# An attention and feed-forward kernel: late query pairs head by head, one first-layer tile later, early query tails in one slot

## The chip, the cores and the metric

The kernel runs on one core of a Trainium2 chip. The metric is the time of one execution in microseconds on the device; several runs are taken and the median is given. TensorE (PE in the profile) multiplies matrices, VectorE (DVE) and ScalarE (ACT) work on elements, GpSimd (POOL) only fills a few tiles here, and SyncE (SP) issues nearly all DMAs from one queue, in order.

## The reference

Two parts in a row: a kernelised attention over 8 batches, 8 heads, 576 tokens and 64 dimensions, then a gated feed-forward layer (FFN) over the 4608 tokens with 512 model dimensions and 1536 hidden ones.

```python
def phi(x):
    proj = np.einsum('bhsd,df->bhsf', x, w_phi)                     # 64 -> 128
    proj = proj - np.max(np.abs(proj), axis=-1, keepdims=True)
    return np.concatenate([np.exp(proj), np.exp(-proj)], axis=-1)   # 256 features
q_p, k_p = (phi(q), phi(k))
kv = np.einsum('bhsf,bhsd->bhfd', k_p, v)
z = np.sum(k_p, axis=2)
num = np.einsum('bhsf,bhfd->bhsd', q_p, kv)
den = np.einsum('bhsf,bhf->bhs', q_p, z)[..., None] + 1e-06
x = (num / den)  # heads side by side: [4608, 512]
g = x @ w_gate
out = (g * (1.0 / (1.0 + np.exp(-g)))) * (x @ w_val) @ w_out
```
Everything is float32. w_gate, w_val and w_out arrive as float64.

## The kernel before

**Attention** goes by pairs of heads: 32 pairs (8 batches, 4 pairs each), made by `attention(i, rank)`. The first 8 are "early": they multiply in plain float32, keep queries with tokens on the partitions, and are double-buffered. The other 24 are "late" (`split`): each float32 operand is taken apart into a rounded part and a remainder (`qh`, `ql`, `kvh`, `kvl`), and there is one set of their buffers.

- Keys: 576 tokens are four tiles of 128 and a rest of 64. `K_GROUPS` makes two groups of two tiles and a tail. In the tail both heads' last 64 tokens share one tile of 128 columns: head 0's rows stand in the first 64 columns, head 1's in the last 64, the rest of `kin` is zero there, and the weight `wst` (w_phi twice, one above the other) projects it to 128 features.
- Early queries: `SLOTS` lists five tiles, and the last starts at token 448, so it takes 64 tokens a second time. Each tile is projected with `wbd` (w_phi twice on the diagonal, 256 columns, both heads), L284; VectorE takes the largest magnitude (L477) and subtracts it (L482), TensorE turns it (L493, one block per head and tile), ScalarE makes the two exponentials (L504).
- Late queries stay features by tokens: rounded part and remainder (L513, L515), projection per head, copies (L528), a 32x32 transpose per head (L533). From there on both heads go in one step: the maximum (L537), six small steps that carry it over the partition groups (L540 to L545), its spreading by a transpose (L549), the subtraction (L551), two exponentials (L553, L554), the rounded copies `qh` (L564) and the remainders `ql` (L567).
- Numerators: products of the query features with `kvs` or `kvh`, `kvl`, in four pieces (two parts of 288 tokens, two heads), copied by L592 and L594, then divided (L601 to L605) and laid into the FFN's input `xh`, `xl` (L617, L619).

**FFN** goes by chunks c of 384 tokens (12) and hidden tiles f of 128 (12). `first(c, f)` is one first-layer tile: 24 products into the two banks `gv` (L284), tanh (L700), two VectorE steps (L702, L705). `parts` makes `hh` and `hl` (L725, L726). `second(c, f)` is 9 products into the three banks `o` (L284); after f = 11 each bank is copied to one of two `osb` buffers (L766) and stored. Chunks 0 to 2 (`EARLY`) share one pass over the weights: for each f, `first` of all three chunks; chunk 0's `second` follows at once, put off by one tile (`put_off` holds one `second` back and issues the one before), and the results of chunks 1 and 2 go to DRAM (`keep`, L712) and come back later (`fetch`, L717). The low parts of w_out for those two chunks are loaded into buffers that the first layer no longer needs (`low_parts_at_rest`, L650).

The weights are turned from float64 into two parts by `weight_piece` (L304 to L325), 36 pieces, on VectorE and ScalarE.

**Order.** Every step is given to a planner (`Plan`) with an engine, a cost, what it waits for and a rank. It runs through time on these costs and issues each engine's instructions in the order in which they would start, lowest rank first; hardware queues keep that order. FFN products have the last rank on TensorE and are chained one after the other in the code's order (`product`); the FFN's steps on the other engines have the first rank. Weights' pieces rank at 3.0, 5.0 and 6.5 to 7.6, pair i at i. Where TensorE has nothing in the plan, it gets a product of zeros (L817 to L821), until chunk 0's last `second` is issued.

Of the kernel before, what the change touches and what calls it, by code (L numbers as in the profile page):

```python
# [29 lines left out]

SLOTS = [0, 128, 256, 384, 448]
Q_GROUPS = [(0, 2), (2, 4), (4, 5)]

K_GROUPS = [(0, 2), (2, 4), (4, 5)]
SK = 5 * P
# [133 lines left out]
def dve(n):  # L169
    return 150 + 1.04 * n  # L170
# [14 lines left out]
def pe32(n):  # L185
    return 2 * max(112, 0.85 * n)
# [3 lines left out]
def favor_attention_moe(ctx: ExitStack, tc: tile.TileContext, qT, kT, v, w_phi, wg, wv, wo, out):  # L190
# [80 lines left out]
    for h in range(2):  # L271
        nc.gpsimd.memset(vf[0][h * D:(h + 1) * D, 4, 1 - h], 0.0)
        nc.gpsimd.memset(kin[0][h * D:(h + 1) * D, 4 * P + (1 - h) * D:4 * P + (2 - h) * D], 0.0)

# [68 lines left out]
    def attention(i, rank):  # L343
# [6 lines left out]
        sets = 2 if early else 1  # L350
        use = lambda name: [last.get((name, i - sets))]

# [27 lines left out]
        kv_steps = []  # L380
        for g, (t0, t1) in enumerate(K_GROUPS):

# [80 lines left out]
        if early:  # L463
            for g, (t0, t1) in enumerate(Q_GROUPS):
# [4 lines left out]
                view = lambda key=key, w=w: work[plan.bank[key]][:, :w * 256].rearrange("p (t f) -> p t f", f=NF)  # L469

                def project(t0=t0, t1=t1, key=key):
# [4 lines left out]
                pj = add("PE", w * pe32(256), project, [q_in], rank, take=key)  # L476
                mx = add("DVE", dve(256 * w), lambda w=w, m=m, view=view: vec.tensor_reduce(  # L477
                    out=m[:, 4:4 + 2 * w], in_=view(), axis=AX.X, op=ALU.max, apply_absolute_value=True),
                    [pj, last.get(("qm", n - len(km)))], rank)

                def centre(w=w, m=m, view=view, y=y):
                    vec.tensor_tensor(  # L482
                        out=y[:, :2 * w], in0=view(), op=ALU.subtract,
                        in1=m[:, 4:4 + 2 * w].rearrange("p (n o) -> p n o", o=1).broadcast_to([P, 2 * w, NF]))

                qc = add("DVE", dve(256 * w), centre, [mx, last.get(("qy", n - 2))], rank, give=key)
                last["qm", n] = qc

                def turn(w=w, y=y, key2=key2):
                    o = work[plan.bank[key2]]  # L490
                    for h in range(2):
                        for t in range(w):
                            nc.tensor.transpose(o[:, (h * w + t) * P:(h * w + t + 1) * P], y[:, 2 * t + h], ident)  # L493

                tn = add("PE", 2 * w * 108, turn, [qc], rank, take=key2)
                last["qy", n] = tn

                skip = P - (S - 4 * P) if t1 == len(SLOTS) else 0
                size = w * P - skip

                def exponential(k, t0=t0, w=w, skip=skip, size=size, key2=key2):
                    x = work[plan.bank[key2]][:, :2 * w * P].rearrange("p (h s) -> p h s", h=2)[:, :, skip:]
                    at = SLOTS[t0] + skip
                    nc.scalar.activation((qe, qx)[k][j][:, :, at:at + size], x, AF.Exp, scale=-1.0 if k else 1.0)  # L504

                f0 = add("ACT", act(2 * size), lambda f=exponential: f(0), [tn, *use("qe"), *use("qx")], rank)
                f1 = add("ACT", act(2 * size), lambda f=exponential: f(1), [f0], rank, give=key2)
            last["qin", i] = pj
        else:
            copies, q_lo = [], []  # L510
            for h in range(2):
                ra, rb = rows(h)
                hi = add("ACT", act(S), lambda h=h, ra=ra: nc.scalar.copy(q_parts()[ra, h], qin[j][ra]),  # L513
                         [q_in, last.get(("qs", h, i - 1)), *first_late("qx", "qe")], rank)
                lo = add("DVE", dve(S), lambda h=h, ra=ra, rb=rb: vec.tensor_tensor(  # L515
                    out=q_parts()[rb, h], in0=qin[j][ra], in1=q_parts()[ra, h], op=ALU.subtract), [hi], rank)
                q_lo.append(lo)
                for part in range(2):
                    key = ("q", i, h, part)
                    c = slice(part * SH, (part + 1) * SH)  # L520

                    def project(h=h, c=c, key=key):
                        acc = work[plan.bank[key]][:, :SH]
                        x = q_parts()[:, h, c]
                        matmuls([(acc, wst_hi, x, True, False), (acc, wst_lo, x, False, True)])

                    pj = add("PE", 2 * pe(SH), project, [lo], rank, take=key)
                    copies.append(add("ACT", act(SH), lambda h=h, c=c, key=key: nc.scalar.copy(  # L528
                        qx[j][:, h, c], work[plan.bank[key]][:, :SH]), [pj, *use("qx")], rank, give=key))
                last["qs", h, i] = pj  # L530
# [4 lines left out]

            def largest():
                vec.tensor_reduce(out=qm, in_=blocks(qe[j]), axis=AX.X, op=ALU.max, apply_absolute_value=True)  # L537

            def over_groups():
# [9 lines left out]
            back = add("DVE", dve(2 * S), lambda: vec.transpose(  # L549
                blocks(qe[j]), qu.rearrange("p (a o) -> p a o", o=1).broadcast_to([P, 2 * NBL, 32])), [mg], rank)  # L550
            qc = add("DVE", dve(2 * S), lambda: vec.tensor_tensor(out=flat(qx[j]), in0=flat(qx[j]), in1=flat(qe[j]),  # L551
                                                                  op=ALU.subtract), [back], rank)
            f0 = add("ACT", act(2 * S), lambda: nc.scalar.activation(flat(qe[j]), flat(qx[j]), AF.Exp), [qc], rank)  # L553
            f1 = add("ACT", act(2 * S), lambda: nc.scalar.activation(flat(qx[j]), flat(qx[j]), AF.Exp, scale=-1.0), [f0], rank)  # L554

        done = [f1]
        if split:
            done = []
            for k in range(2):
                part = (qe, qx)[k][j]  # L560

                def rounded(k=k, part=part):
                    take_over()
                    nc.scalar.copy(flat(qh[k]), flat(part))  # L564

                g0 = add("ACT", act(2 * S), rounded, [(f0, f1)[k], last.get(("nu", i - 1)), *weights_done], rank)
                done += [g0, add("DVE", dve(2 * S), lambda k=k, part=part: vec.tensor_tensor(  # L567
                    out=flat(ql[k]), in0=flat(part), in1=flat(qh[k]), op=ALU.subtract), [g0, f1], rank)]


        copied = []
# [28 lines left out]
        wide = lambda t: t.rearrange("p (a j) -> p a j", j=32)  # L600
        t0 = add("DVE", dve(S), lambda: vec.transpose(turned, den), [*copied, *done], rank)  # L601
        t1 = add("DVE", 260, lambda: vec.reciprocal(rc, wide(turned)[:, :, 0]), [t0], rank)
# [3 lines left out]
        last["qe", i] = t1  # L606
        last["qx", i] = done[-1] if split else nu

# [264 lines left out]
```

## The time and the profile before

| | |
|---|---|
| median of 3 runs | 1282.01 us (1281.12 to 1282.61) |
| the profiled execution | 1281.95 us |
| its span, first to last instruction | 1280.2 us |
| mean granted TensorE clock | 0.996 |
| instructions | 19566 |
| TensorE, weight loads, VectorE, ScalarE busy | 1265.3, 1191.8, 869.2, 642.2 us |
| bytes moved by DMA | 168.13 MB, 131 GB/s |

The profile is of one execution. Times in its rows are us from the span's start unless marked ns. A row of a group of instructions gives line, engine, operation, output and inputs by the program's names, shapes, count, then the total busy time in us and the mean in ns of one, then the engine's idle time before them and what ended it. A row of the timeline gives start, length, engine and line, and in brackets the idle time before it and what ended that. TensorE's products overlap: the length of one is more than the distance to the next, so a cost on TensorE is the distance of two starts. Line numbers are those of the listing above.

### The profile page before, as it was taken

To read this page: it belongs to the slowest core of one execution; us is meant where nothing else is said; L and a number is where in the kernel's file an instruction comes from. 1 tells how busy PE (TensorE), PEld (TensorE's weight loads), DVE (VectorE), ACT (ScalarE), POOL (GpSimd) and SP (SyncE) were. 2 spreads that over 40 slices of the span, in tenths; PEclk is the share of its full clock that TensorE was granted. 3 is DMA by queue.
4 is the path that set the end of the run, shared out by engine and by line. 5 is a ranking of instruction groups with operands and counts; after the bars stand their busy time and mean duration, and the time that the engine had idled before them with its cause. 6 is when DMAs were issued, how large, how long until landed. Compare 5 with 4: busy or idle time off the path is not lost.

```text
span 1280.2 us, 19566 instructions
## 1 busy us (share of the span) xinstructions
PE 1265.3 (99%) x7440; PEld 1191.8 (93%) x7440; DVE 869.2 (68%) x1554; ACT 642.2 (50%) x1287; POOL 1.2 (0%) x11
## 2 busy tenths in 40 slices
PE   9999999999999999999999999999999999999998
PEld 8897899999889999999999999999999999999998
DVE  7998999998787777762777787742477877322222
ACT  5877433336676666531656665531455565221211
POOL 0000000000000000000000000000000000000000
PEclk9999999999899999999999999999999999999999
DMA  5443355543564434444433443444444442443443
GB/s 146 123 121 99 126 179 176 173 163 120 170 195 149 121 102 119 135 126 124 142 107 106 115 140 106 123 151 123 122 129 118 112 132 86 123 148 124 148 123 107
DMA packets 110829, 168.13 MB, mean 131 GB/s; under 512 B 51472, under 2 KB 58128, under 8 KB 110736
## 3 DMA queue, kind: packets, MB, share of 16 engines
q1 hardware_dynamic: 110272, 166.63, 43.6%
q8 instruction: 58, 0.95, 0.3%
q14 instruction: 35, 0.29, 0.1%
q10 hardware_dynamic: 464, 0.26, 0.1%
HBM read 143.26 MB, written 23.59 MB: 130 GB/s over the span
## 4 chain that ended last, share of the span: by engine, by line
PE 93%; DVE 5%; ACT 1%; issue 1%; DMA 1%; SPq 0%; DVEq 0%
PE gv L284 47%; PE o L284 25%; PE work L284 12%; PE kv L431 8%; PE kv L424 1%; PE o L493 0%; DVE kp L411 0%; DVE qy L482 0%; DMA shared<-in_wg_dram 0%; DVE km L406 0%; DVE km L477 0%; DVE qe L549 0%; DVE hl L726 0%; DMA wbd<-in_w_phi_dram 0%; DVE xl L619 0%
## 5 line engine op out<-in xcount | busy, mean ns | idle before, releaser
L284 PE MATMUL gv<-xh,w_hi 128*128 128x384 f32 x1152 | 388.7, 337 | 2.7 <-DVE th L702 2.7
L284 PE MATMUL gv<-xh,w_lo 128*128 128x384 f32 x1152 | 386.9, 336 | 0.0
L284 PE MATMUL gv<-xl,w_hi 128*128 128x384 f32 x1152 | 386.2, 335 | 0.0
L284 PEld LDWEIGHTS gv<-xh,w_hi 128*128 128x128 f32 x1152 | 216.5, 188 | 8.1 <-DVE th L702 3.4
L284 PEld LDWEIGHTS gv<-xl,w_hi 128*128 128x128 f32 x1152 | 216.5, 188 | 4.8
L284 PEld LDWEIGHTS gv<-xh,w_lo 128*128 128x128 f32 x1152 | 216.2, 188 | 0.0
L700 ACT ACTIVATE th<-gv 128x384 f32<-128x384 f32 x144 | 70.6, 490 | 271.0 <-PE gv L284 266.6
L702 DVE SCALAR_TENSOR_TENSOR th<-th,gv 128x384 f32<-128x384 f32 x144 | 79.1, 549 | 147.6 <-ACT th L700 146.8
L284 PE MATMUL o<-w_hi,hl 128*128 128x512 f32 x432 | 171.0, 396 | 0.7 <-DVE hl L726 0.7
L284 PE MATMUL o<-w_hi,hh 128*128 128x512 f32 x432 | 170.7, 395 | 0.0
L284 PE MATMUL o<-w_lo,hh 128*128 128x512 f32 x432 | 170.0, 394 | 0.0
L725 ACT CAST hh<-th 128x384 fp32r<-128x384 f32 x144 | 73.8, 512 | 161.9 <-DVE th L705 150.5
L431 PEld LDWEIGHTS kv<-vf,kp 128*128 128x128 f32 x1024 | 122.9, 194 | 5.0 <-ACT kp L415 2.4
L431 PE MATMUL kv<-vf,kp 128*128 128x66 f32 x1024 | 122.8, 275 | 3.0 <-ACT kp L415 2.0
L705 DVE TENSOR_TENSOR th<-th,gv 128x384 f32<-128x384 f32 x144 | 79.1, 549 | 68.8 <-PE gv L284 66.7
L601 DVE STREAM_TRANSPOSE qe<-den 128x576 f32<-128x576 f32 x32 | 24.9, 778 | 118.7 <-ACT den L594 118.6
L726 DVE TENSOR_TENSOR hl<-th,hh 128x384 fp32r<-128x384 f32 x144 | 79.0, 548 | 32.9 <-ACT hh L725 32.4
L284 PEld LDWEIGHTS o<-w_hi,hl 128*128 128x128 f32 x432 | 81.2, 188 | 19.9 <-DVE hl L726 1.3
L284 PEld LDWEIGHTS o<-w_hi,hh 128*128 128x128 f32 x432 | 81.6, 189 | 11.7 <-ACT osb L766 0.4
L284 PEld LDWEIGHTS o<-w_lo,hh 128*128 128x128 f32 x432 | 81.3, 188 | 11.5
L592 ACT COPY num<-work 64x288 f32<-64x288 f32 x103 | 40.5, 393 | 58.5 <-PE work L284 57.6
L284 PE MATMUL work<-qh,kvh 128*128 128x288 f32 x192 | 61.4, 320 | 0.0
(123 smaller groups left out, 1844.8 us busy)
## 6 DMA issues: line engine op xcount, KB each, us to landing
w_lo<-wlo_dram SPq DMA_DIRECT2D x108, 512.0 KB, 3.6
w_lo<-wlo_dram SPq DMA_DIRECT2D x132, 256.0 KB, 3.0
qin<-in_qT_dram SPq DMA_DIRECT2D x32, 288.0 KB, 2.8
wlo_dram<-w_lo SPq DMA_DIRECT2D x36, 256.0 KB, 2.2
out_dram<-osb SPq DMA_DIRECT2D x35, 256.0 KB, 3.3
kin<-in_kT_dram SPq DMA_DIRECT2D x32, 256.0 KB, 3.0
vf<-in_v_dram SPq DMA_DIRECT2D x64, 128.0 KB, 2.8
shared<-in_wg_dram SPq DMA_DIRECT2D x12, 512.0 KB, 3.5
```

Of the source, the lines that this page charges most:

```text
L284: nc.tensor.matmul(o, l, r, start=a, stop=z)
L424: nc.tensor.matmul(ps_kv[:, 2 * k * D2:2 * (k + 1) * D2], room[:, 0, k], vf[j][:, 4].rearrange("p h d -> p (h d)"), start=False, stop=k == 1)
L431: nc.tensor.matmul(o, room[:, 2 * (t - t0) + h, k], vf[j][:, t, h], start=t + h + k == 0, stop=False)
L592: copied.append(add("ACT", act(SH), lambda key=key, ra=ra, c=c: nc.scalar.copy(num[ra, c], work[plan.bank[key]][ra, :SH]), [nu, free], rank))
L601: t0 = add("DVE", dve(S), lambda: vec.transpose(turned, den), [*copied, *done], rank)
L700: s1 = add("ACT", act(CH), lambda: nc.scalar.activation(t_, ps_gv[0][:, :CH], AF.Tanh, scale=0.5), [ends[0], th_free[j]], FIRST)
L702: s2 = add("DVE", dve(CH), lambda: nc.vector.scalar_tensor_tensor(out=t_, in0=t_, scalar=1.0, in1=ps_gv[0][:, :CH], op0=ALU.add, op1=ALU.m ...
L705: s3 = add("DVE", dve(CH), lambda: nc.vector.tensor_tensor(out=t_, in0=t_, in1=ps_gv[1][:, :CH], op=ALU.mult), [s2, ends[1]], FIRST)
L725: s4 = add("ACT", act(CH), lambda: nc.scalar.copy(hh[b], th[j]), [made, hid_free[b]], FIRST)
L726: s5 = add("DVE", dve(CH), lambda: nc.vector.tensor_tensor(out=hl[b], in0=th[j], in1=hh[b], op=ALU.subtract), [s4], FIRST)
```

## The change

Three edits.

1. Early queries take the keys' grouping (`GROUPS` for both). Their last slot is one tile with both heads' last 64 tokens: `qin` grows to 640 columns with zeros laid at the start, each early pair's queries are loaded by three DMAs (256 KB and two of 16 KB) where there was one, and the tail is projected with `wst` to 128 columns and turned as one block. It is exponentiated as before, 64 tokens for each head.
2. Late pairs' steps from the maximum on are made once per head (L537, L549, L551, L553, L554, L564, L567), and so are the waits: the numerators go head by head and wait for their own head alone. The six small steps stay for both heads. The chain of numerators is now written out (each waits for the one before).
3. In the last f of the pass over the weights the held-back `second(0, 11)` is issued before `first(2, 11)`, not after it.

```diff
-Q_GROUPS = [(0, 2), (2, 4), (4, 5)]
-K_GROUPS = [(0, 2), (2, 4), (4, 5)]
+GROUPS = [(0, 2), (2, 4), (4, 5)]
...
-    kin, qin = [sb("kin", [P, SK])] * 2, [sb("qin", [P, S])] * 2
+    kin, qin = [sb("kin", [P, SK])] * 2, [sb("qin", [P, SK])] * 2
...
+        for t in (kin[0], qin[0]):
+            nc.gpsimd.memset(t[h * D:(h + 1) * D, 4 * P + (1 - h) * D:4 * P + (2 - h) * D], 0.0)
...
-        q_in = add("SP", P * S * 4, lambda: nc.sync.dma_start(qin[j], qT[b, pr]), [last.get(("qin", i - 1))], rank)
+        if early:
+            q_in = [add("SP", P * 4 * P * 4, lambda: nc.sync.dma_start(qin[j][:, :4 * P], qT[b, pr, :, :4 * P]),
+                        [last.get(("qin", i - 1))], rank)]
+            q_in += [add("SP", P * P, lambda r=slice(h * D, (h + 1) * D), c=4 * P + h * D: nc.sync.dma_start(
+                qin[j][r, c:c + D], qT[b, pr, r, 4 * P:]), [last.get(("qin", i - 1))], rank) for h in range(2)]
...
+                u = 1 if tail else 2 * w
...
-                        matmuls([(o[:, (t - t0) * 256:(t - t0 + 1) * 256], qin[j][:, SLOTS[t]:SLOTS[t] + P], wbd, True, True)])
+                        x = qin[j][:, t * P:(t + 1) * P]
+                        matmuls([(o[:, :NF], x, wst, True, True) if tail else
+                                 (o[:, (t - t0) * 256:(t - t0 + 1) * 256], x, wbd, True, True)])
...
-            mx = add("DVE", dve(2 * S), largest, turns, rank)
-            mg = add("DVE", 6 * 170, over_groups, [mx], rank)
+            mx = [add("DVE", dve(S), f, [turns[h]], rank) for h, f in enumerate(per_head(largest))]
+            mg = add("DVE", 6 * 170, over_groups, [*mx, last.get(("back", i - 1))], rank)
+            back = [add("DVE", dve(S), f, [mg], rank) for f in per_head(lambda h: vec.transpose(
...
+            qc = [add("DVE", dve(S), f, [back[h]], rank) for h, f in enumerate(per_head(lambda h: vec.tensor_tensor(
...
+            f0 = [add("ACT", act(S), f, [qc[h]], rank) for h, f in enumerate(per_head(lambda h: nc.scalar.activation(
...
+            f1 = [add("ACT", act(S), f, [f0[h]], rank) for h, f in enumerate(per_head(lambda h: nc.scalar.activation(
...
+            for h in range(2):
+                for k in range(2):
...
+                    g0 = add("ACT", act(S), rounded, [(f0, f1)[k][h], last.get(("nu", i - 1)), *weights_done], rank)
+                    done[h] += [g0, add("DVE", dve(S), lambda k=k, h=h, part=part: vec.tensor_tensor(
...
-        for part in range(2):
-            for h in range(2):
+        for h in range(2):
+            for part in range(2):
...
-                nu = add("PE", 6 * pe(SH) if split else 2 * pe32(SH), numerators, [*done, *kvc], rank, take=key)
+                nu = add("PE", 6 * pe(SH) if split else 2 * pe32(SH), numerators, [*done[h], *kvc, nu], rank, take=key)
...
         for c in range(EARLY):
+            if c == EARLY - 1 and f == NFT - 1:
+                put_off()
             j, h = first(c, f, low)
```

More of the change, by code (lines that the diff above doesn't have):

```diff
@@ L463, in attention @@
         if early:
-            for g, (t0, t1) in enumerate(Q_GROUPS):
+            for g, (t0, t1) in enumerate(GROUPS):
+                tail = t1 == 5
                 w = t1 - t0
+                u = 1 if tail else 2 * w
                 n = 3 * i + g
@@ L479, in attention, with centre @@
+                pj = add("PE", pe32(NF) if tail else w * pe32(256), project, q_in, rank, take=key)
+                mx = add("DVE", dve(u * NF), lambda u=u, m=m, view=view: vec.tensor_reduce(
+                    out=m[:, 4:4 + u], in_=view(), axis=AX.X, op=ALU.max, apply_absolute_value=True),
                     [pj, last.get(("qm", n - len(km)))], rank)
[L481 removed]
+                def centre(u=u, m=m, view=view, y=y):
                     vec.tensor_tensor(
[L483 to L484 removed]
@@ L486, in attention, with turn @@
-                qc = add("DVE", dve(256 * w), centre, [mx, last.get(("qy", n - 2))], rank, give=key)
+                        out=y[:, :u], in0=view(), op=ALU.subtract,
+                        in1=m[:, 4:4 + u].rearrange("p (n o) -> p n o", o=1).broadcast_to([P, u, NF]))
+                qc = add("DVE", dve(u * NF), centre, [mx, last.get(("qy", n - 2))], rank, give=key)
                 last["qm", n] = qc
-                def turn(w=w, y=y, key2=key2):
+                def turn(w=w, y=y, key2=key2, tail=tail):
@@ L490, in turn @@
                     o = work[plan.bank[key2]]
-                    for h in range(2):
+                    for h in range(1 if tail else 2):
                         for t in range(w):
                             nc.tensor.transpose(o[:, (h * w + t) * P:(h * w + t + 1) * P], y[:, 2 * t + h], ident)
-                tn = add("PE", 2 * w * 108, turn, [qc], rank, take=key2)
+                tn = add("PE", u * 108, turn, [qc], rank, take=key2)
                 last["qy", n] = tn
-                skip = P - (S - 4 * P) if t1 == len(SLOTS) else 0
@@ L499, in attention, with exponential @@
[L499 to L504, printed above, removed]
+                size = D if tail else w * P
+                def exponential(k, t0=t0, size=size, key2=key2):
+                    x = work[plan.bank[key2]][:, :2 * size].rearrange("p (h s) -> p h s", h=2)
+                    nc.scalar.activation((qe, qx)[k][j][:, :, t0 * P:t0 * P + size], x, AF.Exp, scale=-1.0 if k else 1.0)
@@ L512, in attention @@
                 ra, rb = rows(h)
-                hi = add("ACT", act(S), lambda h=h, ra=ra: nc.scalar.copy(q_parts()[ra, h], qin[j][ra]),
-                         [q_in, last.get(("qs", h, i - 1)), *first_late("qx", "qe")], rank)
+                hi = add("ACT", act(S), lambda h=h, ra=ra: nc.scalar.copy(q_parts()[ra, h], qin[j][ra, :S]),
+                         [*q_in, last.get(("qs", h, i - 1)), *first_late("qx", "qe")], rank)
                 lo = add("DVE", dve(S), lambda h=h, ra=ra, rb=rb: vec.tensor_tensor(
-                    out=q_parts()[rb, h], in0=qin[j][ra], in1=q_parts()[ra, h], op=ALU.subtract), [hi], rank)
+                    out=q_parts()[rb, h], in0=qin[j][ra, :S], in1=q_parts()[ra, h], op=ALU.subtract), [hi], rank)
                 q_lo.append(lo)
@@ L574, in attention @@
+        copied, nu = [], None
+        for h in range(2):
+            for part in range(2):
                 key = ("n", i, h, part)
@@ L600, in attention @@
         wide = lambda t: t.rearrange("p (a j) -> p a j", j=32)
-        t0 = add("DVE", dve(S), lambda: vec.transpose(turned, den), [*copied, *done], rank)
+        t0 = add("DVE", dve(S), lambda: vec.transpose(turned, den), [*copied, *done[0], *done[1]], rank)
         t1 = add("DVE", 260, lambda: vec.reciprocal(rc, wide(turned)[:, :, 0]), [t0], rank)
@@ L606, in attention @@
         last["qe", i] = t1
-        last["qx", i] = done[-1] if split else nu
+        last["qx", i], last["qx'", i] = (done[0][-1], done[1][-1]) if split else (nu, None)
         odd = b % 2
```

51 lines of the change are left out of this document (23 added, 28 removed).

## The prediction

> **What bounds the kernel now.** I read the busy table and the chain of waits on the page first, then a table of busy time by stage, then TensorE's own waits.
>
> ```profile
> span 1280.2 us, 19566 instructions
> ...
> PE 1265.3 (99%) x7440; PEld 1191.8 (93%) x7440; DVE 869.2 (68%) x1554; ACT 642.2 (50%) x1287; POOL 1.2 (0%) x11
> ...
> PE 93%; DVE 5%; ACT 1%; issue 1%; DMA 1%; SPq 0%; DVEq 0%
> ```
> TensorE is busy 99% of the span and carries 93% of the chain, so only two things can move the end: less TensorE work, or fewer holes in it. The stage table shows where the holes are (its columns: stretch, length, busy time of each engine with its instructions, granted clock, DMA share, GB/s).
>
> ```profile
> 16.00:104.00 88.00, 87.92 (x541) 78.89 (x540) 82.37 (x154) 69.14 (x163) 0.00 (x0) 0.99 0.43 121
> 133.00:145.00 12.00, 9.28 (x56) 8.65 (x56) 11.40 (x21) 5.10 (x10) 0.00 (x0) 1.00 0.21 60
> 316.00:332.00 16.00, 13.55 (x71) 12.00 (x70) 8.57 (x13) 11.84 (x21) 0.00 (x0) 0.79 0.61 205
> 404.00:1116.00 712.00, 712.00 (x4322) 679.64 (x4321) 475.19 (x824) 379.92 (x747) 0.00 (x0) 1.00 0.42 122
> ```
> From 404 us on nothing is idle on TensorE and VectorE has a third of its time free: whatever per-head steps do there, the end follows TensorE's work. The holes that the change can touch lie at 133 to 145 and at 316 to 332, where the granted clock too is 0.79. The early pairs (16 to 104) are full on TensorE, with VectorE at 82.37 of 88 close behind.
>
> **The change part by part.**
>
> **Early pairs' last slot.** TensorE projects one 128-wide tile in place of a 256-wide one, and turns one block in place of two.
>
> ```profile
> 58.55 1.03 PE L284 MATMUL o<-wbd,kin 128*128 128x256 f32 x4
> 59.42 0.61 PE L424 MATMUL kv<-vf,kp 128*128 128x132 f32 x4
> ...
> 60.73 0.60 PE L493 MATMUL o<-ident,qy 128*128 128x128 f32 x4
> 61.17 0.39 PE L284 MATMUL work<-wst,kin 128*128 128x128 f32 x2
> 61.39 0.38 PE L493 MATMUL o<-ident,qy 128*128 128x128 f32 x2
> ```
> Durations overlap, so starts are subtracted: four 256-wide passes take 59.42 - 58.55 = 0.87 us, 0.217 each; four turns 61.17 - 60.73 = 0.44, 0.110 each; two 128-wide passes 61.39 - 61.17 = 0.22, 0.110 each. A projection is two passes: saved 2 x (0.217 - 0.110) + 0.110 = 0.32 us a pair, 2.6 us for eight. VectorE's reduction of the tail becomes that of K's tail:
>
> ```profile
> L477 DVE TENSOR_REDUCE km<-o 128x2 f32<-128x256 f32 x7 | 2.9, 414 | 0.0
> L406 DVE TENSOR_REDUCE km<-work 128x1 f32<-128x128 f32 x29 | 8.2, 282 | 1.4 <-PE work L284 1.4
> ```
> 0.13 us saved, and about as much (estimate) in the subtraction of the same columns: 0.26 x 8 = 2.1 us. Both co-limiting engines lose nearly the same, so I let it reach the end for six pairs of eight (pair 0 lies in the start, the last pair's tail beside late work): 0.32 x 6 = 1.9. Bounds: 0 (another engine sets the pace) and 2.6. ScalarE still does 128 outputs per exponential: nothing.
>
> Against it stand 16 more DMAs on SP's queue, two small ones per early pair, ahead of the V loads and of the weights' raw loads, and two more fills on GpSimd before anything reads them.
>
> ```profile
> 326.58 1.11 SPq L358 DMA_DIRECT2D kin<-in_kT_dram  x2
> ...
> kin<-in_kT_dram SPq DMA_DIRECT2D x64, 16.0 KB, 2.6
> ```
> K's tail is loaded this way already: two issues take 1.11 us of SP, and each lands in 2.6 us. So V and weights behind them start 1.1 us later in each early pair. The first pair's V is needed only after its K maxima and exponentials, which covers it; weights run ahead by a pair. Bounds 0 and 1.1 (once, at the start); I take 0.2, off the sum.
>
> **One first-layer tile comes later.** Before: tile (2,11), then second(0,11), then second(1,0). After: second(0,11), tile (2,11), second(1,0). What follows the present order:
>
> ```profile
> 314.66 0.34 PE L284 MATMUL gv<-xh,w_lo 128*128 128x384 f32 x1
> ...
> 317.55 0.33 PE L284 MATMUL work<-wst_hi,ks 128*128 128x128 f32 x1 [0.47 <-DVE kp L411]
> ...
> 320.32 0.40 PE L284 MATMUL work<-qs,wst_hi 128*128 128x288 f32 x1 [0.77 <-DVE qs L515]
> ...
> 322.08 3.91 PE L431 MATMUL kv<-vf,kp 128*128 128x66 f32 x16 [1.22 <-ACT kp L415]
> 325.74 0.59 PE L284 MATMUL work<-qh,kvh 128*128 128x288 f32 x1
> ...
> 328.77 1.96 PE L431 MATMUL kv<-vf,kp 128*128 128x66 f32 x16
> 330.53 0.38 PE L284 MATMUL work<-qh,kvh 128*128 128x288 f32 x1
> ...
> 332.21 0.61 PE L424 MATMUL kv<-vf,kp 128*128 128x132 f32 x4
> ```
> Three holes: 0.47 + 0.77 + 1.22 = 2.46 us. The first sixteen kv products take 3.91 against 1.96 for the next sixteen: 1.95 lost. The first twelve numerators take 328.77 - 325.74 = 3.03 against 332.21 - 330.53 = 1.68: 1.35 lost to the clock. Together 5.8 us. Why there was no other work: second(1,0)'s third token block needs second(0,11)'s third output copied away, and that copy waits for an output buffer.
>
> ```profile
> 316.87 1.06 ACT L766 ACTIVATE osb<-o 128x512 f32<-128x512 f32 x2
> ...
> 324.10 0.60 ACT L766 ACTIVATE osb<-o 128x512 f32<-128x512 f32 x1
> ```
> The third copy is 7.2 us after the first two, because the stores stand behind the loads of low parts:
>
> ```profile
> 313.58 1.84 SPq L650 DMA_DIRECT2D w_lo<-wlo_dram  x4
> ...
> 317.60 0.86 SPq L769 DMA_DIRECT2D out_dram<-osb  x2
> ```
> After the change the first copies come while ScalarE is free, their stores go ahead of the low parts, and tile (2,11) covers them:
>
> ```profile
> 148.89 8.35 PE gv L284 x48
> ...
> w_lo<-wlo_dram SPq DMA_DIRECT2D x132, 256.0 KB, 3.0
> ```
> Two tiles are 48 products and 8.35 us in the chain of waits (start, length, what), so one is 4.2 us, over the copies and the exponentials of the pair in work. What is late next: second(1,0) needs its own low part, whose load the code lists behind tile (2,11). SP issued the first of them 1.25 us before that tile ended (313.58 against 314.66 + 0.17); at 3.0 us to landing (the median above) the hole is 1.8 us, less about 0.6 (estimate) of attention work that stands ready, the K and Q pieces at 317.55 and 320.32: 1.0 to 1.2. I take 1.0, so 4.8 is saved. Bounds: 0, if the load waits for the tile's end and the clock falls again, and 5.8.
>
> The page "TensorE: Matmul & The Clock Gate" of the Trainium skill (What's actually happening) says that the clock halves after an idle window of about 3.4 us. This stretch shows it at 0.79 with no hole over 1.22 us, so the trace does not bear out that a whole window must be idle; by that rule the slow numerators would have another cause, would stay, and the sum would be 3.3 us higher.
>
> **Late pairs head by head.** Five VectorE steps and four ScalarE steps become two each.
>
> ```profile
> L549 DVE STREAM_TRANSPOSE qe<-qu 128x1152 f32<-128x1152 f32 x24 | 33.0, 1373 | 0.2
> L533 DVE STREAM_TRANSPOSE qe<-qx 128x576 f32<-128x576 f32 x48 | 35.8, 761 | 0.7 <-ACT qx L528 0.7
> L564 ACT CAST qh<-qe 128x1152 fp32r<-128x1152 f32 x24 | 27.4, 1142 | 0.0
> L513 ACT CAST qs<-qin 64x576 fp32r<-64x576 f32 x48 | 32.3, 674 | 0.7
> ```
> VectorE: 2 x 0.761 - 1.373 = 0.15 a step, 0.75 a pair, 18 us in all. ScalarE: 2 x 0.674 - 1.142 = 0.21, 0.8 a pair, 20 us in all. Cover: both have a third or more free from 404 on. Without it, FFN steps queue behind them. For them a step of half the length is the gain:
>
> ```profile
> 140.47 1.36 DVE L551 TENSOR_TENSOR qx<-qx,qe 128x1152 f32<-128x1152 f32 x1
> ...
> PE gv L284 <- DVE th L702: 2.7, 2, 2.1
> ...
> PE o L284 <- DVE hl L726: 0.7, 1, 0.7
> ```
> TensorE waits 2.1 us for L702, which stands behind a 1.36 us subtraction of both heads. Behind one of 0.75 (half of L551, as L533 is to L549) it starts 0.6 to 1.36 earlier; I take 0.7, bounds -0.7 (behind two halves and a transpose) and 1.4. The 0.7 at L726 is of the same kind; I take 0.3, bounds -0.3 and 0.7. From 404 on: 0, bounds -0.5 and +0.5, since no hole is there to close.
>
> **Sum.** 1.9 - 0.2 + 4.8 + 0.7 + 0.3 = 7.5 us. The profiled execution took 1281.95 us (its span and 1.75 around it), 0.06 under the median of 1282.01, so 1274.5 us. Best ends: 2.6 + 5.8 + 1.4 + 0.7 + 0.5 = 11.0, 1271.0. The queues are laid out anew, so padding products may go too:
>
> ```profile
> L821 PE MATMUL o<-nil x14: 279/280/283, 157.1 to 310.6; 128*128 128x256 f32 x14
> ```
> 14 at up to 0.28 us are 3.9 more; all of it together is unlikely, so the range starts at 1268.
>
> **The rivals.**
>
> *The slow clock comes again* with the hole that is left: 1.95 + 1.35 = 3.3 us stay, 1277.8. For it: the clock fell at holes of 0.47 to 1.22. Against: only one hole is left.
>
> *The early edit is hidden* by VectorE's order or by loads in SP's queue: 1276.2. For it: VectorE at 94%, 16 more issues. Against: it loses 2.1 us as well.
>
> *The hole only moves.* The low parts wait for the tile's end; 3.0 to landing, then the clock: nothing of 5.8 is saved, 1281.95 - 2.7 = 1279.3. For it: the code lists them behind the tile. Against: the first two overwrite a buffer that tile (2,10) read last.
>
> *Slower: the attention chain becomes the bound.* FFN moves ahead of attention by 5.1 us, and chunk 4 needs pair 15:
>
> ```profile
> 510.99 0.82 DVE L619 TENSOR_TENSOR xl<-num,xh 128x192 fp32r<-128x192 f32 x2
> ...
> 522.57 0.39 PE L284 MATMUL gv<-xh,w_hi 128*128 128x384 f32 x1
> ```
> Ready at 511.8, used at 522.6: 10.8 us of slack. If the split lengthens each of pairs 8 to 15 by d, TensorE waits once 8d exceeds 10.8 - 5.1, from 0.7 us. Slower than before by 0.2% needs 8d = 10.8 + 2.4 + 2.6, d = 2.0 us (2.4 = 1.7 + 0.7 is what attention gains too); at 2.5 the end is 1281.95 - 2.4 + (20 - 10.8) = 1288.8. All splits in series give only 0.75 + 0.8 = 1.55, so it needs FFN steps queued between the halves; 8 x 1.55 - 10.8 = 1.6 gives 1281.2, no change. Against it: one head's numerators (1.6 us) can run while the other is prepared.
>
> That the tile is not moved at all is excluded: each FFN product waits for the one before it in the code's order.
>
> **How the numbers follow.** Chances: forecast 0.55, with a range of its own of 1271 to 1277; slow clock 0.10; early edit hidden 0.12; hole moves 0.13; attention binds without loss 0.05; slower 0.05. About 0.2% (2.6 us) is what can be told from no change, so faster means under 1279.4: 0.55 + 0.10 + 0.12 + two thirds of 0.13 = 0.86; same 0.09; slower 0.05. The range 1268 to 1280 leaves out the last two cases and little more.
>
> **What would show it.** Early: 16 projections of 128x128 from qin and 72 turns, not 80; the stage ends some 2 us earlier. Tile: no hole beyond 1 us after second(0,11), all three output copies within some 4 us, granted clock 1.00 there. Heads: 48 steps in place of 24 at about 0.75 us, TensorE's wait for L702 near 1.4 us, no hole before chunks 3 and 4. The prediction is wrong if the new order opens a hole where none was, most likely where chunk 4 begins or where the low parts land.

## The result, and the profile after

The changed kernel takes 1274.96 us (median of 5 runs, 1273.64 to 1276.63) where the kernel before, in 5 runs beside it, takes 1282.01: a ratio of 0.9949, 95% interval 0.9938 to 0.9960, 7.05 us less. The forecast was 1274.5. A second visit (e10, below) gave 1275.96 us and a ratio of 0.9953 (0.9939 to 0.9966). The time agrees with the forecast. The experiments show that the terms behind it do not stand as they were argued, so a part of the agreement is luck.

The page of the changed kernel's profile, the lines that answer to the first ones of before:

```profile
span 1271.9 us, 19806 instructions
...
PE 1258.4 (99%) x7432; PEld 1186.9 (93%) x7432; DVE 875.1 (69%) x1674; ACT 651.6 (51%) x1383; POOL 1.3 (0%) x13
...
PE 92%; DVE 5%; ACT 1%; DMA 1%; issue 0%; SPq 0%; DVEq 0%; ACTq 0%
```

TensorE still sets the end; it is busy 6.9 us less. The same stages as before (columns: stretch, length, busy time of PE, PEld, DVE, ACT, POOL with instructions, granted clock, DMA share, GB/s; the third stretch begins 4 us earlier because the work does):

```profile
16.00:104.00 88.00, 87.03 (x540) 77.95 (x538) 81.96 (x158) 69.03 (x164) 0.00 (x0) 0.99 0.43 124
132.00:144.00 12.00, 10.78 (x64) 10.33 (x64) 11.55 (x26) 2.76 (x5) 0.00 (x0) 1.00 0.42 129
312.00:328.00 16.00, 13.00 (x83) 11.25 (x81) 12.09 (x20) 11.68 (x23) 0.00 (x0) 1.00 0.63 202
404.00:1116.00 712.00, 712.00 (x4319) 679.12 (x4318) 483.40 (x923) 386.94 (x826) 0.00 (x0) 1.00 0.41 122
```

In the third stretch TensorE is idle for 3.0 us, more than the 2.45 us of before, but the clock is 1.00 and not 0.79. The timeline of TensorE there (start, length, and in brackets the idle time before it and what ended it):

```profile
312.56 0.40 PE L282 MATMUL o<-w_hi,hh 128*128 128x512 f32 x1
314.35 0.50 PE L282 MATMUL o<-w_lo,hh 128*128 128x512 f32 x1 [1.39 <-DMA w_lo<-wlo_dram]
314.69 0.40 PE L282 MATMUL o<-w_hi,hl 128*128 128x512 f32 x1
316.70 0.33 PE L282 MATMUL work<-wst_hi,ks 128*128 128x128 f32 x1 [1.62 <-DVE kp L415]
...
322.83 1.90 PE L435 MATMUL kv<-vf,kp 128*128 128x66 f32 x16
```

So three holes of 0.47, 0.77 and 1.22 us became two of 1.39 and 1.62 us: nothing was closed, but the sixteen kv products now take 1.90 us and not 3.91. The row for tanh's product in the changed kernel's table of TensorE's waits (us in total, times, longest) and the instructions that the first two edits promised:

```profile
PE gv L282 <- DVE th L717: 1.5, 2, 1.2
```
```profile
L502 PE MATMUL o<-ident,qy 128*128 128x128 f32 x72 | 11.7, 283 | 0.0
...
L282 PE MATMUL o<-wst,qin 128*128 128x128 f32 x14 | 2.7, 274 | 0.0
...
L282 PE MATMUL work<-wst,qin 128*128 128x128 f32 x2 | 0.4, 274 | 0.0
L559 DVE STREAM_TRANSPOSE qe<-qu 128x576 f32<-128x576 f32 x48 | 36.1, 766 | 0.4
L579 ACT CAST qh<-qe 128x576 fp32r<-128x576 f32 x48 | 32.0, 667 | 0.0
```

72 turns and 14 + 2 narrow projections; 48 steps of 0.77 and 0.67 us. The wait for tanh's product (L702 before, L717 now) fell from 2.1 to 1.2 us, the one for `hl` is gone.

**How the runs are compared.** All kernels below scatter by some us, and the scatter goes with the granted clock: the 72 runs of the kernel before that have their clock on record take 1278.8 us on average at 0.999, 1280.3 at 0.997, 1283.3 at 0.995 and 1285.0 at 0.993. One common slope fitted over all 184 runs, with a level of its own for each kernel, is 1.13 us for each 0.001 of clock, and 0.7 us of scatter are left. So each difference is split: "equal clock" is the difference in level, "clock" the rest. Means are used, since they add up.

| kernel | runs | median, us | ratio (95%) | mean clock | mean against before | equal clock | clock |
|---|---|---|---|---|---|---|---|
| before | 72 | 1282.38 | | 0.9958 | | | |
| changed (two visits) | 10 | 1275.65 | 0.9949, 0.9953 | 0.9969 | -6.3 | -5.0 | -1.3 |
| e1 tail alone | 11 | 1277.17 | 0.9961 (0.9950, 0.9973) | 0.9956 | -4.6 | -4.7 | +0.2 |
| e2 heads alone | 12 | 1280.44 | 0.9989 (0.9979, 1.0000) | 0.9954 | -1.5 | -1.9 | +0.4 |
| e3 tile alone | 12 | 1281.65 | 0.9995 (0.9984, 1.0007) | 0.9957 | -0.5 | -0.6 | +0.1 |
| e5 tail, order of before | 12 | 1282.64 | 1.0009 (1.0000, 1.0018) | 0.9947 | +0.3 | -0.9 | +1.3 |
| e6 without tile | 12 | 1279.58 | 0.9980 (0.9970, 0.9989) | 0.9952 | -2.7 | -3.4 | +0.7 |
| e7 without heads | 12 | 1278.76 | 0.9978 (0.9965, 0.9992) | 0.9944 | -3.1 | -4.7 | +1.5 |
| e8 without tail | 12 | 1278.34 | 0.9976 (0.9965, 0.9987) | 0.9960 | -3.5 | -3.3 | -0.3 |
| e9 before, holes filled | 5 | 1277.58 | 0.9960 (0.9947, 0.9972) | 0.9992 | -4.2 | -0.4 | -3.9 |
| e11 changed, filled | 5 | 1272.59 | 0.9920 (0.9908, 0.9933) | 0.9992 | -9.3 | -5.4 | -3.9 |
| e4 early loads | 5 | 1273.65 | 0.9928 (0.9915, 0.9942) | 0.9986 | -8.7 | -5.5 | -3.2 |
| e12 early loads, filled | 4 | 1271.66 | 0.9912 (0.9898, 0.9925) | 0.9998 | -10.4 | -5.9 | -4.5 |

The differences in level have a standard error of about 0.2 us (12 runs) to 0.4 us (4 runs).

A second table splits each profiled span by stage, with half of TensorE's busy time in the half-rate windows taken out (a window lasts 3.41 us and so costs up to 1.7). The marks are the starts of the first product of the tiles (0,0) and (2,0), of chunk 3, and the end.

| net us | to (0,0) | to (2,0) | to chunk 3 | to the end | sum | windows taken out, us |
|---|---|---|---|---|---|---|
| before | 44.7 | 87.9 | 265.8 | 876.6 | 1275.0 | 5.1 |
| e5 tail, order of before | 44.6 | 86.6 | 266.2 | 877.5 | 1274.9 | 4.9 |
| e1 tail alone | 44.8 | 86.3 | 263.4 | 877.1 | 1271.6 | 3.3 |
| e8 without tail | 45.0 | 89.3 | 259.2 | 878.3 | 1271.9 | 5.0 |
| e7 without heads | 44.4 | 86.3 | 262.6 | 876.6 | 1269.9 | 5.1 |
| changed | 43.8 | 86.3 | 261.0 | 879.1 | 1270.2 | 1.7 |

### The profile page after: what moved, and what is told of

Its sections match the earlier page's. It is cut to its first block, busy times and chain, and to the rows that moved or that the text cites. A ratio compares the mean times of both kernels' runs of the same rounds, so it can differ in the third digit from the quotient of the medians.

```text
span 1271.9 us, 19806 instructions
## 1 busy us (share of the span) xinstructions
PE 1258.4 (99%) x7432; PEld 1186.9 (93%) x7432; DVE 875.1 (69%) x1674; ACT 651.6 (51%) x1383; POOL 1.3 (0%) x13
## 4 chain that ended last, share of the span: by engine, by line
PE 92%; DVE 5%; ACT 1%; DMA 1%; issue 0%; SPq 0%; DVEq 0%; ACTq 0%
PE gv L282 47%; PE o L282 25%; PE work L282 12%; PE kv L435 7%; PE kv L428 1%; DVE kp L415 1%; DVE km L410 0%; ACT den L609 0%; DVE qy L491 0%; ACT num L607 0%; PE o L502 0%; DVE den L618 0%; DVE qe L616 0%; DVE num L620 0%; DMA shared<-in_wg_dram 0%
## 5 line engine op out<-in xcount | busy, mean ns | idle before, releaser
L717 DVE SCALAR_TENSOR_TENSOR th<-th,gv 128x384 f32<-128x384 f32 x144 | 79.1, 549 | 148.2 <-ACT th L715 146.6
```

Source lines behind the costliest of these rows:

```text
L717: s2 = add("DVE", dve(CH), lambda: nc.vector.scalar_tensor_tensor(out=t_, in0=t_, scalar=1.0, in1=ps_gv[0][:, :CH], op0=ALU.add, op1=ALU.m ...
```

## The experiments

**One edit at a time: e1, e2, e3.** Each is the kernel before with the lines of one edit.

```diff
e1  -        q_in = add("SP", P * S * 4, lambda: nc.sync.dma_start(qin[j], qT[b, pr]), ...
    +            q_in += [add("SP", P * P, lambda r=..., c=...: nc.sync.dma_start(qin[j][r, c:c + D], qT[b, pr, r, 4 * P:]), ...
    +                        matmuls([(o[:, :NF], x, wst, True, True) if tail else ...
e2  -            mx = add("DVE", dve(2 * S), largest, turns, rank)
    +            mx = [add("DVE", dve(S), f, [turns[h]], rank) for h, f in enumerate(per_head(largest))]
e3  +            if c == EARLY - 1 and f == NFT - 1:
    +                put_off()
```

> The kernel before with edit 1 alone (the tail slot of early queries, its three loads). Theory, by the prediction's own term: TensorE loses 0.32 us in each of six to eight early pairs, the loads cost 0.2: 1.7 to 2.4 us less, near 1280; pair 7's inputs to the FFN ready some 2 us before 131.5 us, the stretch at 316 to 332 with its holes and its low clock as before. Rival, the early edit is hidden (VectorE or SP's queue sets the pace): within 0.5 us of the kernel before, pair 7 ready at 131 or later.

> The kernel before with edit 2 alone (late pairs' query steps head by head). Theory: it shortens what FFN steps queue behind, so TensorE's 2.1 us wait at 140 us shrinks to about 1.2 (as in the changed kernel) and the 0.7 us hole at 374 closes, together 1.5 to 2.5 us less; the holes at 316 to 332 stay within 1 us of 5.8, since the third output copy still comes late: near 1280. Rival, the per-head chain itself closes the holes at 316 to 332 by bringing the first head's numerators forward: 3 us or more saved there, total near 1276. Rival on the other side: 18 us more VectorE work and 20 us more ScalarE work delay FFN steps: no gain or a loss.

> The kernel before with edit 3 alone (tile (2,11) after second(0,11)). Theory: the third output copy comes within 4 us of the first and the 5.8 us lost at 316 to 332 shrink to 3 (a hole of about 1.4 for the first low part and one for attention behind it), granted clock 1.00: 3 us less, near 1279; all before 300 us as before. Rival, the holes only move: within 0.5 us of the kernel before. Rival, the loss is closed whole when VectorE's steps are not split (no K tail waiting behind split halves): 5 us less, near 1277.

Measured: -4.6, -1.5 and -0.5 us. The small tail edit brings most, nearly three times its term and more than either side expected. e2 comes out near the 1280 us of its theory: TensorE's longest wait for tanh's product fell from 2.1 to 0.8 us, while in its late stage a hole of 3.0 us opened. The tile edit, 4.8 us in the sum, brings nothing in the time that can be told from zero. TensorE's waits in its late stage, e3:

```profile
315.82 0.33 PE L284 MATMUL work<-wst_hi,ks 128*128 128x128 f32 x1 [1.25 <-DVE kp L411]
319.12 0.80 PE L284 MATMUL o<-w_lo,hh 128*128 128x512 f32 x1 [2.46 <-DMA w_lo<-wlo_dram]
```

3.71 us of holes where there were 2.46, and the second product's length of 0.80 us (0.50 in the changed kernel, 0.40 elsewhere) shows the clock already halved. Alone, the hole only moves: the third rival.

**The tail edit without its new order: e5.** The planner is told the old costs and one load step, so every other instruction stays in the order of before. Two of its edits, against e1:

```diff
-                pj = add("PE", pe32(NF) if tail else w * pe32(256), project, q_in, rank, take=key)
+                pj = add("PE", w * pe32(256), project, q_in, rank, take=key)
...
-                tn = add("PE", u * 108, turn, [qc], rank, take=key2)
+                tn = add("PE", 2 * w * 108, turn, [qc], rank, take=key2)
```

> The early pairs' cut of the last query slot (128 columns instead of 256, two turns fewer per early block, loads in the same step) with every other instruction left in the order of the kernel before. Theory (the cut alone is worth what its removed work shows, and the rest of what the early edit alone gave came from the new order that followed it): 1279.4 to 1280.3 us, 1.7 to 2.6 us under the kernel before; the late stages, measured from the first tile of chunk 0's projections, as in the kernel before, with its hole at 368 to 375 us still there. Rival (the cut itself gives all 5 us, since starting 2 us earlier closes holes further on): 1277 us, and the hole at 368 to 375 us is gone. Second rival (the removed work was hidden): within 0.5 us of the kernel before.

Measured: 1282.64 us, +0.3 in the mean, -0.9 at equal clock. The time is that of the second rival, but its reason is not: from (0,0) to (2,0) the stage table has 86.6 us net against 87.9, so the removed work was not hidden, and the cut reaches the end of its stage with 1.3 us, near the 1.7 of the sum. What takes it back comes through the clock, at two places. The first is the start, and there the loads in SP's queue are the cause. SP's issue of the first raw weights and TensorE's wait ahead of the first pair's second group of kv products, in the kernel before and then in e5, with ScalarE's step between them:

```profile
6.34 0.58 SPq L304 DMA_DIRECT2D shared<-in_wg_dram  x1
...
12.26 0.44 PE L431 MATMUL kv<-vf,kp 128*128 128x66 f32 x2 [0.79 <-ACT kp L415]
```
```profile
7.60 0.58 SPq L302 DMA_DIRECT2D shared<-in_wg_dram  x1
...
11.85 0.66 ACT L304 ACTIVATE shared<-shared 128x512 f32<-128x512 f32 x1 [2.50 <-DMA shared<-in_wg_dram]
...
13.09 3.92 PE L438 MATMUL kv<-vf,kp 128*128 128x66 f32 x16 [1.91 <-ACT kp L422]
```

The two small loads put off the raw weights by 1.3 us. ScalarE's first step on these weights stands in its order ahead of the exponential that the kv products wait for, so TensorE's wait grows, and the sixteen products behind it run at half rate (3.92 us). It is the same in the other kernels: in the seven profiles with the tail edit and no zeros at 11 us, one or two half-rate windows each lie in the first 21 us (10 in all), and tile (0,0) starts at 46.9 us on average; in the five without the edit there is one in all, and it starts at 44.8.

The second place is the wait for tanh's product at 140 us, which is as long as before; the same stretch cut at two of the clock's windows, in the kernel before and then in e5:

```profile
137.74:141.16 3.42, 2.52 (x15) 2.20 (x13) 3.15 (x9) 0.49 (x1) 0.00 (x0) 1.00 0.00 0
141.16:144.57 3.41, 2.23 (x13) 2.23 (x14) 3.31 (x6) 2.34 (x2) 0.00 (x0) 1.00 0.17 59
```
```profile
138.92:142.33 3.41, 1.33 (x8) 1.01 (x6) 3.30 (x4) 0.91 (x2) 0.00 (x0) 1.00 0.00 0
142.33:145.74 3.41, 3.40 (x11) 3.40 (x12) 3.28 (x6) 1.92 (x2) 0.00 (x0) 0.50 0.37 132
```

Before, an edge of the windows splits the hole (idle 0.90 and 1.18 us) and the clock stays at 1.00. In e5 all of it lies in one window (idle 2.08 us) and the next runs at 0.50: 1.7 us lost. Where the edges fall changes from run to run, so at this place it is a matter of odds. e5's mean clock is 0.9947 against 0.9958; how much of that either place makes up was not measured. The rest of e1's gain (its level is 3.8 us under that of e5) is the order that the planner lays with the new costs and load steps: the stretch from (2,0) to chunk 3 takes 263.4 us net in e1 and 266.2 in e5.

**One edit left out: e6, e7, e8.** The changed kernel without the lines of e3, e2 and e1.

> The early cut and the head-by-head steps, without the later first-layer tile. Theory (the three edits add): 1282.0 - 5.0 - 1.4 = 1275.6 us, so the tile edit brings only 0.6 us to the full change, and the stretch of 304 to 335 us loses 5.6 us or less. Rival (the tile edit pays only in the company of the others, since the stretch at 304 to 335 us loses 3.6 us in the full change and 5.6 to 8.0 us in each edit alone): 1277.5 to 1279 us, with a loss of 5.6 to 7 us in that stretch.

> The early cut and the later first-layer tile, without the head-by-head steps. Theory (the three edits add): 1282.0 - 5.0 - 0.6 = 1276.4 us, the wait of 2 us at about 132 to 140 us still there. Rival (the tile needs both others): 1277.5 to 1279 us, with a loss of 5.6 us or more in the stretch at 304 to 335 us.

> The head-by-head steps and the later first-layer tile, without the early cut. Theory (the three edits add): 1282.0 - 1.4 - 0.6 = 1280.0 us. Rival (heads and tile together close the stretch at 304 to 335 us, which neither closes alone): 1277 us, with a loss there under 4 us.

Measured: 1279.58, 1278.76 and 1278.34 us. None meets the sum of the single edits in the median (1275.6, 1276.4, 1280.0 were expected), e6 and e7 fall behind it and e8 is ahead. e7 lies in the range of its rival, e6 0.6 us beyond it, and e8 between its two. Put in last, an edit is worth, by the table (changed minus without):

| put in last | mean | equal clock | clock |
|---|---|---|---|
| tail (e8) | -2.7 | -1.7 | -1.0 |
| tile (e6) | -3.5 | -1.6 | -2.0 |
| heads (e7) | -3.1 | -0.3 | -2.8 |

The standard error at equal clock is 0.3 us here, so what the heads are worth there cannot be told from nothing. Most of what tile and heads are worth comes through the clock. e6 has the longest hole of the late stage in any of these kernels, with e2's, and it waits for the same VectorE step as the changed kernel:

```profile
319.52 0.33 PE L282 MATMUL work<-wst_hi,ks 128*128 128x128 f32 x1 [3.01 <-DVE kp L415]
321.93 0.79 PE L282 MATMUL o<-w_hi,hh 128*128 128x512 f32 x1 [1.86 <-ACT osb L781]
```

That step stands at the end of a row of VectorE steps with hardly a gap. VectorE in the changed kernel:

```profile
311.69 0.77 DVE L559 STREAM_TRANSPOSE qe<-qu 128x576 f32<-128x576 f32 x1
312.77 0.55 DVE L720 TENSOR_TENSOR th<-th,gv 128x384 f32<-128x384 f32 x1 [0.31 <-PE gv L282]
313.24 0.77 DVE L559 STREAM_TRANSPOSE qe<-qu 128x576 f32<-128x576 f32 x1
313.93 1.38 DVE L562 TENSOR_TENSOR qx<-qx,qe 128x576 f32<-128x576 f32 x2
315.24 0.68 DVE L410 TENSOR_REDUCE km<-work 128x4 f32<-128x512 f32 x1
315.95 0.69 DVE L415 TENSOR_TENSOR kp<-work,km 128x512 f32<-128x512 f32 x1
```

One gap of 0.31 us in five us, and in the three windows from 311.87 to 322.11 us (last section) VectorE is busy for 9.83 of 10.24 us; before, it was for 9.94 of 10.24 from 311.83 on. There VectorE, beside the load of the low part, is what TensorE runs into, and none of the three edits takes work from it there. That the holes moved and were not closed for this reason is read from the traces; no run takes work from VectorE in that stretch.

**Filling the holes with zeros: e9, e11.** e9 is the kernel before with 23 products of zeros (12, 4 and 7) where TensorE sat idle; the order of all else is unchanged.

```diff
+    def still(bank, n, new=False):
+        for _ in range(n):
+            nc.tensor.matmul(bank[:, :2 * P].rearrange("p (a n) -> p a n", n=P), nil, zeros, start=new, stop=new)
...
+                if (c, f, a, k) == (2, 0, 1, NK - 1):
+                    still(ps_o[0], 12, True)
...
+                if (c, f, t) == (1, 0, 1):
+                    still(ps_o[0], 4)
...
+                        if (i, h, c.start) == (10, 0, 0):
+                            still(ps_o[0], 7)
```

> The kernel before with 23 matmuls of zeros put where TensorE sat idle: 12 ahead of the wait of 2.1 us at 140 us, 4 and 7 ahead of the holes of 0.77 and 1.22 us at 319 and 321 us. Nothing else moves, no wait gets shorter. Theory (the half-rate windows of the clock, 3.41 us long, follow a window of that grid in which TensorE was idle for more than about 1.7 us, so they go when the holes are filled): no window under 1.00 between 20 us and the last few us, mean clock 0.997 to 0.999 where the runs of the kernel before have 0.9958 on average, and 1279 to 1280.3 us, 1.7 to 3 us under the kernel before. Rival (the half-rate windows come from the load before, or from chance): 0.996 again and within 0.6 us of the kernel before, or slower by the zeros that overrun a wait.

> The changed kernel with 34 matmuls of zeros in its holes: 7 at 11 us, 8 at 137 us, 9 and 10 at 313 and 315 us; nothing else moves. Theory of the idle windows: clock 0.998 to 0.9995 and 1272.5 to 1273.8 us, 1 to 2.5 us under the changed kernel. Rival (the changed kernel's holes are already too short for a half-rate window past 20 us, and those at the start come with the first loads): 0.997 and within 0.6 us of the changed kernel.

Measured: 1277.58 us, ratio 0.9960 (0.9947 to 0.9972), at a mean clock of 0.9992: the theory, with more gain than its range of 1279 to 1280.3 us allowed. The time went without any wait being removed. The late stage of e9, the answer to the rows of before in the prediction:

```profile
317.29 0.63 PE L280 MATMUL o<-nil 128*128 128x256 f32 x4
318.23 0.40 PE L289 MATMUL work<-qs,wst_hi 128*128 128x288 f32 x1 [0.31 <-DVE qs L520]
...
318.60 0.99 PE L280 MATMUL o<-nil 128*128 128x256 f32 x7
319.98 0.44 PE L436 MATMUL kv<-vf,kp 128*128 128x66 f32 x2 [0.39 <-ACT kp L420]
320.64 1.78 PE L436 MATMUL kv<-vf,kp 128*128 128x66 f32 x14 [0.23 <-ACT kp L421]
322.23 0.38 PE L289 MATMUL work<-qh,kvh 128*128 128x288 f32 x1
...
323.91 1.90 PE L436 MATMUL kv<-vf,kp 128*128 128x66 f32 x16
```

The products still wait for the same steps, but the sixteen kv products take 322.23 - 319.98 = 2.25 us with a wait of 0.23 in it, and the twelve numerators 323.91 - 322.23 = 1.68 us, full rate; before they took 3.91 and 3.03. So 1.95 + 1.35 us of the kernel before were indeed the clock, as the prediction read them, and idle time brings it on. In the changed kernel a like filling (e11, 34 products) gives 1272.59 us at 0.9992, as its theory had it, 0.4 us under the changed kernel at equal clock and 2.6 through the clock.

**The changed kernel again: e10.** No edit.

> The changed kernel once more, beside the others: 1274.4 to 1275.6 us, clock 0.9972 on average, if its five runs were typical. If the clock was lucky in them, 0.9958 and 1276.4 us.

Measured: 1275.96 us at 0.9966. Together with the first five runs 0.9969: better than the 0.9958 of before, by 1.3 us, and far from 0.9992. The time lies between the two that were expected.

**A better version: e4, e12.** In e4 the loads of w_out's low parts for chunks 1 and 2 wait only for the last reader of the buffer that they overwrite.

```diff
-            rest_user[k] = list(lo_user[0][-1] + lo_user[0][-2] if k < 2 * LO_SETS else lo_user[1][-1] + lo_user[1][-2])
+            one = [u for n, u in enumerate(lo_user[0]) if n % LO_SETS == k // 2]
+            rest_user[k] = list(one[-1] if k < 2 * LO_SETS else lo_user[1][-1] + lo_user[1][-2])
```

> The changed kernel, and the first two low parts of w_out for chunks 1 and 2 wait only for the tile that last read their own buffer, (2,10), and no longer for (2,11). Theory: the hole left in the changed kernel is the load issued late (TensorE waits 1.39 us for w_lo at 314, then 1.62 us for VectorE's K step because it comes to that step early): both close or shrink, 1.5 to 3 us less than the changed kernel, 1272 to 1273.5. Rival, attention bound: chunk 3 needs pair 11, ready at 394.5 in the changed kernel and used at 397.5, so 3 us of slack eat the gain and a new hole stands near 395: 0 to 1 us less. Rival, the second hole is VectorE's own order and stays whole: 1.4 us less.

e4 takes 1273.65 us. The wait for `w_lo` is gone, and the idle time is found elsewhere, in one hole ahead of a numerator that waits for ScalarE to free its bank:

```profile
323.90 0.40 PE L282 MATMUL work<-qh,kvh 128*128 128x288 f32 x1 [2.28 <-ACT den L609]
```

At equal clock it stands 0.5 us under the changed kernel, less than can be told; its mean clock is 0.9986. So most of what e4 gains comes through the clock, and not from the shorter wait as its theory had it. e12 adds zeros in the three holes left (7 at 11 us, 8 at 137 us, 14 ahead of that numerator).

> The changed kernel with the later loads of low parts waiting for the last reader of their own buffers alone (as in e4), and 29 matmuls of zeros: 7 at 11 us, 8 at 137 us, 14 ahead of the hole of 2.3 us at 321 us. Theory of the idle windows: 0.999 and 1272.3 to 1273.3 us. Rival: as e4, 1273.7 us at 0.9986, since its hole was one window at most already.

```profile
core 0: 1269.5 us, clock 1.000
```

1271.66 us, ratio 0.9912 (0.9898 to 0.9925): the best of all, 0.6 us better than the range that was expected, and 10.7 us under the median of all runs of the kernel before.

## Why the prediction was right, and where it was not

Of the 7.5 us in the sum, 3.3 were clock and 4.2 were work and holes. By the means of the runs it was 1.3 through the clock and 5.0 at equal clock. The total came out; the parts did not.

- **Tail, 1.7 us net: the cut was right in size at its place, the load term was not.** Net of the clock, (0,0) to (2,0) takes 86.3 us in the changed kernel against 87.9, and 86.3 to 86.6 in every kernel of the stage table with this edit; put in last it is worth 1.7 us at equal clock. The load term was taken as 0.2, with 1.1 as its bound, because the weights "run ahead by a pair". In the first pair they do not, as the rows of e5 show: ScalarE meets them ahead of the second exponential of the first pair's keys. The wait ahead of the first pair's second sixteen kv products, in the profiles without zeros there, is 0.0 to 1.1 us in the five kernels without the edit (mean 0.5) and 0.9 to 1.9 in the seven with it (mean 1.4). Net of the clock the start takes 43.8 to 45.0 us either way, but with the half-rate windows it ends 2.1 us later in the profiles with the edit. So the loads cost about what the cut saves, and most of it through the clock, which the prediction did not look for at this place. That is the mechanism of its second rival (loads in SP's queue), and e5 has that rival's price. What the prediction also lacked is that the planner lays another order on the new costs: alone, that order was worth 3.8 of e1's 4.7 us at equal clock.
- **Tile, 4.8 us: the step that failed is the hole.** The prediction put the holes down to the output copies and took one of 1.0 us as left. The copies do come together now (first row below), as forecast. But two holes are left, 3.0 us in all, 2.0 more than was taken. One is the low part's load, which opened a hole where none was, at a place that the prediction had named as its sign of being wrong. SP's queue and the groups of these loads in the changed kernel (its window from 300 to 320 us):

```profile
L781 ACT ACTIVATE osb<-o x3: 598/599/602, 305.8 to 308.5; 128x512 f32<-128x512 f32 x3
```
```profile
310.17 2.91 SPq L665 DMA_DIRECT2D w_lo<-wlo_dram  x4
```
```profile
DMA to landing us min/median/max: 2.6/4.1/5.0
```

  SP issued it at 310.17, 2.6 us before the second product would have started (312.56 + 0.23), earlier than assumed, but with 344 GB/s moving in that stretch it took 4.1 us and not 3.0, so TensorE waited 1.39. The other, 1.62 us, is VectorE, which was not in the argument. The 3.3 us of clock in that stage did go in the profiled run. So the outcome is the third rival's mechanism (the hole moves) without the first rival's price (the slow clock comes again), and two kinds of error nearly cancel: on one side 2.0 us more of holes than taken, the loads at the start and a clock that gives less on average, on the other a few us from the new order that were not foreseen. That they cancel is luck.
- **Heads, 1.0 us: right in kind alone, small in company.** TensorE's wait for tanh's product came out at 1.2 us (1.4 was forecast), that for `hl` at nothing. Alone the edit is worth 1.9 us at equal clock, put in last 0.3: the stage table shows "to chunk 3" 1.6 us shorter and "to the end" 2.5 us longer than in e7. That is work that changed sides, not a cost from 404 on, where none was forecast: chunk 3 begins earlier, and 14 more of the attention's products (12 of keys, 2 of queries; `work` has 919 against 905) come after its first product, about 1.7 us. Another 0.8 lies behind the last product (4.4 and 3.6 us; 4.1 in e10, 3.6 in e8). In between TensorE has no idle time in either kernel.
- **The slower rival** needed 2.0 us more per late pair. The pairs come no later: `xl` of pair 7 is ready at 130.6 us and that of pair 15 at 509.3, where it was 131.5 and 511.8. FFN moved ahead by more, so the slack ahead of the fourth group of chunk 4's products fell from 10.8 to 3.6 us, but it did not run out.
- **The clock.** The prediction held, against the page "TensorE: Matmul & The Clock Gate" of the Trainium skill (What's actually happening), that the slow stretch comes from holes far shorter than a window. e9 shows it. What it missed is that the windows come by odds: of 6.3 us in the mean, 1.3 come through the clock, where 3.3 were counted from one execution.

## What to carry to other kernels

Before costing a hole, look at the granted clock beside it: two idle us inside one window of 3.41 us cost up to 1.7 us more for each half-rate window that follows, and products of zeros placed in the hole win that back without touching the wait (4.2 us here, as much as most of the change). A load added at the very start can cost in the same way. When edits go through a planner that lays the queues anew, cost the cut and the new order apart: keep the old order once, and judge each edit by leaving it out of the whole as well as by putting it in alone. Where a hole moves at each edit, find the engine that is busy without gaps in the microseconds ahead of it; that it has to lose work is the next thing to try, which no run here does.

## What the runs showed of the clock

The changes of the granted clock within a trace lie at multiples of 3.41 us from each other, and past the first 20 us nine of the eleven changes to 0.50 follow a window in which TensorE was idle for more than half. Four windows of before, then those of e7 and of the changed kernel (columns as above):

```profile
311.83:315.25 3.42, 3.42 (x21) 3.38 (x20) 3.28 (x7) 0.49 (x1) 0.00 (x0) 1.00 0.48 139
315.25:318.66 3.41, 2.94 (x14) 2.15 (x14) 3.34 (x6) 2.86 (x5) 0.00 (x0) 1.00 0.86 298
318.66:322.07 3.41, 1.43 (x6) 0.67 (x4) 3.32 (x6) 3.38 (x5) 0.00 (x0) 1.00 0.99 338
322.07:325.49 3.42, 3.41 (x15) 3.25 (x16) 1.99 (x4) 3.21 (x6) 0.00 (x0) 0.50 0.65 223
```
```profile
314.87:318.28 3.41, 0.79 (x6) 0.47 (x4) 3.38 (x6) 1.95 (x2) 0.00 (x0) 1.00 0.99 341
318.28:321.69 3.41, 3.41 (x10) 2.32 (x11) 3.31 (x6) 3.38 (x5) 0.00 (x0) 0.50 0.79 275
```
```profile
311.87:315.28 3.41, 1.83 (x8) 1.01 (x7) 3.10 (x6) 0.60 (x1) 0.00 (x0) 1.00 1.03 344
315.28:318.69 3.41, 1.99 (x10) 1.73 (x11) 3.34 (x7) 3.35 (x7) 0.00 (x0) 1.00 0.32 119
318.69:322.11 3.42, 3.42 (x19) 2.91 (x18) 3.39 (x7) 3.10 (x7) 0.00 (x0) 1.00 0.59 188
```

Idle for 1.98 us of 3.41 and for 2.62: half rate follows. Idle for 1.58 and again for 1.42: it does not. In the changed kernel 0.74 us of products stand between its two holes, and in the profiled run an edge of the windows falls into the second. Over the 14 profiled runs, between 20 us and the last windows, nine full-rate windows have 1.85 us or more of idle time, and all nine are followed by half rate; 27 have 1.0 to 1.72, and one is; some 5000 have less, and one is (at 124.6 us in e2, with 0.78). In the first 20 us idle times of 0.9 to 1.6 us were enough, nine times.

The traces suggest why. These nine windows and the one in e2 are alike in one thing: each holds 1.4 to 2.6 us of kv products with 66 columns. If the time of such products is counted as idle by four tenths (an estimate, fitted to the windows of the 14 profiles), all 20 windows that half rate follows have 1.6 us or more, and of some 5100 others only four come as high, none above 1.72. So idle time is not all that counts, it seems, but also what the products in the window are; no run tests it. One to three half-rate windows follow one another; what sets their number stays open.

The page "TensorE: Matmul & The Clock Gate" of the Trainium skill (What's actually happening) says that the activity window is 3413 ns long and runs freely, not from the kernel's start. The traces agree: the spacing is 3.41 us, and the edges lie elsewhere in each run. It also says that the clock falls after at least one idle window. Here 1.85 us of idle time in a window, 54% of it, were enough nine times in nine.
